# A decode backward kernel on Trainium2: PSUM tiles of two banks and copies of 1024 columns, with a rearranged opening and tail of its last stage

## The chip, the cores and the metric

The kernel runs on one core of one Trainium2 chip. The metric is the device time of an execution in microseconds (us), median over the timed runs. The executions of a kernel lie within about half a per cent of their median here. PE is the matmul engine (PEld its weight loads), DVE the vector engine, ACT the scalar engine, POOL and SP are here the queues that issue stores and loads. PSUM is the memory that PE writes into. The kernel divides it into eight pieces of 512 float32 values per partition, called banks here (its pools take 2 + 4 + 1 + 1), and none of its matmuls writes to more than one. In this program DVE or ACT copies each product out of PSUM ("copy" below), and the bank is filled again only after that. The granted clock is the speed at which the chip's throttle lets PE run, as a share of full speed.

"The Trainium skill" is a set of notes on the chip. Where a statement rests on it, the page is named, and the text says whether the trace agrees.

## The reference, cut to what matters

The reference is a forward pass of two attention blocks and two MLP blocks that share their weights, with one new token per sequence and a KV cache of 16384 entries, followed by the gradient of everything.

```
B, Sq, D = 2, 1, 1024;  Hq, Hkv, Sk, Dh = 32, 4, 16384, 128;  F = 3584      # bf16
x = A_x
for layer in (0, 1):
    x = x + attention(layernorm(x), k_cache, v_cache, wq, wo)
    x = x + mlp(layernorm(x), w1, b1, w2, b2)
return x, *grads(A_x, k_cache, v_cache, wq, wo, w1, b1, w2, b2)
```

The outputs that matter here are the gradients of the caches, dK and dV (33.6 MB each), those of the weights (dWq, dWo, dW1, dW2, together 31.5 MB), and the gradient of the input, the second output, 4 KB, which comes last in the data flow: it needs the whole dq (the gradient of the queries), then dq times Wq, then a layer-norm backward.

## The kernel before: the parts that are touched

What matters of the change is in the last stage, from about 735 us on. In it, K and V chunks and quarters of Wq are loaded once more, dq of layer 0 is formed, and all of dK, dV and dW is computed, copied and stored. Products go to four PSUM tiles of one bank each, used in turn. The program sends each copy to DVE or ACT, whichever has less work by its own count.

```python
    X = [px([128, 512], F32, "xm%d" % i) for i in range(4)]      # four tiles, one bank each
    def mx():
        return nxt("x", X)                                       # the next of the four

    def evac_cast(dst, src, n):                                  # one copy, on ACT or DVE
        if pick() == "A":
            S.copy(out=dst, in_=src)
            charge("A", 0.17 + n / 1200.0)
        else:
            V.tensor_copy(out=dst, in_=src)
            charge("D", 0.15 + n / 960.0)

    # in dw_units: one unit of a weight gradient = one product, one copy
                        ps = mx()
                        PE.matmul(ps[:], lhsT=xrows[p:p + 4, (j0 + j) * 128:(j0 + j + 1) * 128],
                                  rhs=yrows[p:p + 4, y0 + c0:y0 + c0 + 512], start=True, stop=True, tile_position=(p, 0))
                        evac_cast(sv_[:, j, c0:c0 + 512], ps[:], 512)

    # in kv_pair: half a chunk of dK or dV = eight products into four tiles, four copies
        pss = [mx() for _ in range(4)]
        for b in range(2):
            for r in range(4):
                PE.matmul(pss[r][:, b * 256:(b + 1) * 256], lhsT=blk[32 * r:32 * r + 32, o + 2 * h + b, :],
                          rhs=Qm[32 * r:32 * r + 32, :, :].rearrange("p a b -> p (a b)"), start=True, stop=True,
                          tile_position=(32 * r, 0))
        for r in range(4):
            evac_cast(sv_[:, 2 * h:2 * h + 2, r], pss[r][:].rearrange("p (b t d) -> p b t d", b=2, t=2), 512)
```

The main loop goes in steps; in the traces below, the products of PE and the copies of DVE and ACT run in the program's order. A step transposes two blocks of V, forms score products, up to two halves of dK or dV, then some dW units, then issues loads.

```python
    while 2 * m < NS + 12 or late or fill or late_pe or m <= max(v_at) + 2:
        ...                       # for k in 0, 1: 8 transposes of V and their copy, 8 score products, halves of dK / dV
        sch.run_slot(1)           # dq products of earlier steps
        step_fill(1 if m < NCH else 5)              # five dW units of 512 columns
        pump(NLD + 3 if m < NCH else NLD, 3)        # loads, as far as SBUF tiles are free
        m += 1
    g0 = attn_in_bwd(0, g1, dn0)                    # the serial end: layer-norm backward,
    col_to_row_f32(g0, DJ, out_1..., "o1")          # rows, the store of the second output
```

A load takes an SBUF tile that a store has freed, if there is one, and otherwise one that a reader has freed (`(by_store or by_read).popleft()`).

Of the kernel before, what the change touches and what calls it, by code (L numbers as in the profile page):

```python
# [23 lines left out]
def kernel(  # L24
# [65 lines left out]
    ps_x = ctx.enter_context(tc.tile_pool(name="ps_x", bufs=4, space=PSUM))  # L90
    ps_acc = ctx.enter_context(tc.tile_pool(name="ps_acc", bufs=1, space=PSUM))
    ps_sm = ctx.enter_context(tc.tile_pool(name="ps_sm", bufs=1, space=PSUM))

# [30 lines left out]
    zero1 = const.tile([128, 1], F32, name="zero1")  # L124
    V.memset(zero1[:], 0.0)
# [69 lines left out]
    def col_to_row_f32(colT, J, dram_out, name):  # L195
        row = wrk.tile([2, J * 128], BF16, name=name + "_row", tag="rowout")
        for j0 in range(0, J, 4):
            ps = pm_([2, 4, 128], F32, name)
            for j in range(4):
                PE.transpose(ps[0:2, j, :], colT[:, j0 + j, :], identf[:])  # L200
            V.tensor_copy(out=row[:, j0 * 128:(j0 + 4) * 128], in_=ps[0:2, :, :].rearrange("p a b -> p (a b)"))
        nc.gpsimd.dma_start(dram_out, row[:])
# [529 lines left out]
    n_all = vec.tile([128, DJ, 4], BF16, name="n_all")  # L732
    o_all = vec.tile([128, HQ, 4], BF16, name="o_all")
    dq_all = vec.tile([128, HQ, 4], BF16, name="dq_all")
    gA_all = vec.tile([128, DJ, 4], BF16, name="gA_all")
    m_all = vec.tile([128, DJ, 4], BF16, name="m_all")
    h_all = vec.tile([128, FJ, 4], BF16, name="h_all")
    dh_all = vec.tile([128, FJ, 4], BF16, name="dh_all")
    gM_all = vec.tile([128, DJ, 4], BF16, name="gM_all")
    V.tensor_copy(out=gM_all[:, :, 2:4], in_=gT4[:])  # L740
# [7 lines left out]
    def attn_layer_fwd(l, xT):  # L748
        y, rstd = ln_fwd(xT[:], f"a{l}")
        V.tensor_copy(out=n_all[:, :, lsl(l)], in_=y[:])  # L750
        qps, _ = w_pass(A_wq, D, HD, "q_ps", xT_bf=n_all[:, :, lsl(l)])
        qT_bf = vec.tile([128, G, 8], BF16, name=f"qT_bf{l}")
        for b in range(2):
            V.tensor_scalar(out=qT_bf[:, b * HKV:(b + 1) * HKV, :].rearrange("p k r -> p (k r)"), in0=qps[:, :, b],
                            scalar1=QSCALE, scalar2=None, op0=ALU.mult)
        rbc = vec.tile([128, G, 8], F32, name=f"rbc{l}")
        oT = vec.tile([128, G, 8], F32, name=f"oT{l}")
        attn_fwd(l, qT_bf, rbc, oT, ALLG)
        for b in range(2):
            V.tensor_copy(out=o_all[:, :, 2 * l + b], in_=oT[:, b * HKV:(b + 1) * HKV, :].rearrange("p k r -> p (k r)"))  # L760
        aps, _ = w_pass(A_wo, HD, D, "a_ps", xT_bf=o_all[:, :, lsl(l)])
        xn = vec.tile([128, DJ, 2], F32, name=f"xA{l}")
        V.tensor_tensor(out=xn[:], in0=aps[:], in1=xT[:], op=ALU.add)
        saved[f"a{l}"] = dict(y=y, rstd=rstd, qT_bf=qT_bf, rbc=rbc, oT=oT)
        return xn

    def mlp_hidden(l, xT):
        y1, rstd1 = ln_fwd(xT[:], f"m{l}a")
        y2, rstd2 = ln_fwd(y1[:], f"m{l}b")
        V.tensor_copy(out=m_all[:, :, lsl(l)], in_=y2[:])  # L770
        hps, _ = w_pass(B_w1, D, F, "h_ps", xT_bf=m_all[:, :, lsl(l)])
# [17 lines left out]
        V.tensor_tensor(out=h_all[:, :, lsl(l)], in0=hh[:], in1=hpre[:], op=ALU.mult)  # L789
# [24 lines left out]
    def mlp_hidden_bwd(l, dhps, ahead=None):  # L814
        d1 = saved[f"m{l}"]["d1"]
        V.tensor_tensor(out=dh_all[:, :, lsl(l)], in0=d1[:], in1=dhps[:], op=ALU.mult)
        if ahead is not None:
            V.tensor_tensor(out=dh_all[:, 4:FJ:5, lsl(l)], in0=d1[:, 4:FJ:5], in1=ahead.dp[:], op=ALU.mult)

    def mlp_in_bwd(l, gT):  # L820
        sv = saved[f"m{l}"]
        _, dmps = w_pass(B_w1, D, F, "dm_ps", gT_bf=dh_all[:, :, lsl(l)])
# [8 lines left out]
    def attn_out_bwd(l, gT):  # L831
        V.tensor_copy(out=gA_all[:, :, lsl(l)], in_=gT[:])
        _, dops = w_pass(A_wo, HD, D, "do_ps", gT_bf=gA_all[:, :, lsl(l)])
        doT_bf = saved[f"a{l}"]["doT_bf"] = vec.tile([128, G, 8], BF16, name=f"doT_bf{l}")
        dof = wrk.tile([128, G, 8], F32, name="dof")
        do_scaled(l, dops, dof)
        do_store(l, dof[:], doT_bf[:])
        delta(l, delta_mm(l, dof))
        return doT_bf
# [74 lines left out]
    fps, dhps = w_pass(B_w2, F, D, "w2a", xT_bf=h_all[:, :, lsl(0)], gT_bf=gM_all[:, :, lsl(1)])  # L914
# [15 lines left out]
    w2b = Ahead(B_w2, F, "w2b", h_all[:, :, lsl(1)], fps)  # L930
# [16 lines left out]
    V.tensor_copy(out=gM_all[:, :, lsl(0)], in_=g2[:])  # L947
    dhps = px([128, 512], F32, "w2b_b")
    turned = 5
    for j in range(4):  # L950
        w2b.products(j, dhps, gM_all[:, :, lsl(0)])
    w2b.spread(gM_all[:, :, lsl(0)])
    w2b.dots(4)
    for j in range(4, FJ):
# [6 lines left out]
        w2b.products(j, dhps, gM_all[:, :, lsl(0)])  # L961
# [86 lines left out]
    _, dmps = w_pass(B_w1, D, F, "dm_ps", gT_bf=dh_all[:, :, lsl(0)],  # L1048
# [13 lines left out]
    V.tensor_copy(out=gA_all[:, :, lsl(0)], in_=g1[:])  # L1062
    dops = px([128, 512], F32, "wob_b")
    for j in range(4):
        wob.products(j, dops, gA_all[:, :, lsl(0)])
    wob.spread(gA_all[:, :, lsl(0)])
# [4 lines left out]
    for j in range(4, wob.J):  # L1071
# [8 lines left out]
        wob.products(j, dops, gA_all[:, :, lsl(0)])  # L1080
# [7 lines left out]
    def rows_unit(srcs, dst, j0):  # L1088

        def u():  # L1090
            tp = mtp()
            n = 0
            for i, (colT, jlo) in srcs.items():
                jn = min(8, colT.shape[1] - jlo)
                n = max(n, jn)
                for j in range(jn):
                    PE.transpose(tp[32 * i:32 * i + 4, j, :], colT[:, jlo + j, :], ident[:], tile_position=(0, 32 * i))  # L1097
            lo, hi = 32 * min(srcs), 32 * max(srcs) + 4
            evac_bf16(dst[lo:hi, j0 * 128:(j0 + n) * 128], tp[lo:hi, 0:n, :].rearrange("p a b -> p (a b)"), n * 128)
# [3 lines left out]
    X = [px([128, 512], F32, "xm%d" % i) for i in range(4)]  # L1103
# [11 lines left out]

    def n_free():
# [4 lines left out]

    def load_tile():
        return (by_store or by_read).popleft()
# [25 lines left out]
    def dw_units(xrows, yrows, i, chunks, y0, ny, out_of):  # L1149

        p = 32 * i
        box = {}
        units = []
        for j0, rb in chunks:
            for j in range(rb):
                for c0 in range(0, ny, 512):
                    def u(j0=j0, rb=rb, j=j, c0=c0):
                        if j == 0 and c0 == 0:
                            box["t"] = new_home()
                        sv_ = box["t"][:, 0:rb * ny].rearrange("p (j n) -> p j n", j=rb)  # L1160
                        ps = mx()
                        PE.matmul(ps[:], lhsT=xrows[p:p + 4, (j0 + j) * 128:(j0 + j + 1) * 128],  # L1162
                                  rhs=yrows[p:p + 4, y0 + c0:y0 + c0 + 512], start=True, stop=True, tile_position=(p, 0))
                        evac_cast(sv_[:, j, c0:c0 + 512], ps[:], 512)
                        if j == rb - 1 and c0 + 512 >= ny:
# [8 lines left out]
    for i in range(NCH, NC + 1):  # L1174
        if i < NC:
            if chunks[i] != (XG, 0):
                jobs.append(("V",) + chunks[i])
            if i % (2 * NCH) == NCH:
# [33 lines left out]
    fill.append(rows_unit({0: (gM_all, 0), 1: (m_all, 0), 2: (gA_all, 0), 3: (n_all, 0)}, rowsB, 0))  # L1212
    for j0 in range(0, HQ, 8):
        srcs = {0: (h_all, j0), 1: (dh_all, j0), 2: (o_all, j0)}
        fill.append(rows_unit({i: v for i, v in srcs.items() if j0 < v[0].shape[1]}, rowsA, j0))
# [9 lines left out]
    late, late_pe = deque(), deque()  # L1225
# [7 lines left out]
    def kv_pair(w, i, h):  # L1233
# [7 lines left out]
        pss = [mx() for _ in range(4)]  # L1241
        for b in range(2):
            for r in range(4):
                PE.matmul(pss[r][:, b * 256:(b + 1) * 256], lhsT=blk[32 * r:32 * r + 32, o + 2 * h + b, :],  # L1244
                          rhs=Qm[32 * r:32 * r + 32, :, :].rearrange("p a b -> p (a b)"), start=True, stop=True,
                          tile_position=(32 * r, 0))
        for r in range(4):
            evac_cast(sv_[:, 2 * h:2 * h + 2, r], pss[r][:].rearrange("p (b t d) -> p b t d", b=2, t=2), 512)
# [12 lines left out]

    def quarter(kv):

        quarters[kv][1]()
        late_pe.append(quarters[kv][3])
        late.append(rows_unit({3: (dq_all, kv * 8)}, rowsA, kv * 8))
# [43 lines left out]
    def score0(s):  # L1310
# [7 lines left out]
        if c == 0:  # L1318
            open_dq(g)
            if order.index(g) % 2 == 1:  # L1320
                quarter_loads(g % HKV)
        ds0(i, dps["t"][:])
        sch.later(1, lambda: dq_quad(i, 0))
        sch.later(2, lambda: dq_quad(i, 1))
        if c == NCH - 1:
            sch.later(2, accs[g].evac)
            sch.later(3, accs[g].reduce)

    def step_fill(n):
        for k in range(n):  # L1330
            for q in ((late, fill) if k % 2 == 0 else (fill, late)):
                if q and q[0].ready():
# [6 lines left out]

    def fixed_tp(i):  # L1340
        t = pt([128, 8, 128], BF16, "tpm%d" % i)
        S.copy(out=t[:].bitcast(F32), in_=zero1[:].to_broadcast([128, 512]))
        return t
# [21 lines left out]
    odp = {1: kept_scores(1, sm_dp())}  # L1365
# [4 lines left out]
    odp[0] = kept_scores(0, tp_dp())  # L1370
# [6 lines left out]
    odp[3] = kept_scores(3, sm_dp())  # L1377
# [9 lines left out]
    TP.extend(fixed_tp(i) for i in range(2))  # L1387
# [3 lines left out]
    pump(NLD + 3, 4)  # L1391
# [5 lines left out]
    NS = (NC - NCH) * NB  # L1397
    m = 0
    while 2 * m < NS + 12 or late or fill or late_pe or m <= max(v_at) + 2:
# [6 lines left out]
        for k in range(2):  # L1406
# [17 lines left out]
            if late_pe and (k == 1 or s >= NS):  # L1424
                late_pe.popleft()()
            at, w, m_ = ((k_at, "K", m - 1), (v_at, "V", m))[k]
            for h in range(2):
                if at.get(m_ - h) is not None:
                    kv_pair(w, at[m_ - h], h)
        for f in qs:  # L1430
            f()
# [3 lines left out]
        step_fill(1 if m < NCH else 5)  # L1435
        pump(NLD + 3 if m < NCH else NLD, 3)
        m += 1
    g0 = attn_in_bwd(0, g1, dn0)
    col_to_row_f32(g0, DJ, out_1.rearrange("b s d -> (b s) d"), "o1")
# [30 lines left out]
```

## Time and profile before

The median was 1144.42 us of 3 runs.

| reading of before | value | where |
|---|---|---|
| bytes moved, mean rate | 449.30 MB, 394 GB/s | first page, DMA |
| busy share PE / DVE / ACT | 84% / 56% / 50% | first page, part 1 |
| DMA rate 735 to 820 / 820 to 1100 / 1100 to end | 328 / 422 / 298 GB/s | windows |
| a copy of 512 columns, DVE / ACT | 686 / 594 ns | groups of instructions |

These are lines of the first page of before: busy time of each engine, then, in 40 equal slices of the span, the clock granted to PE in tenths of full speed, the busy share of the DMA engines in tenths, and the rate.

```profile
PE 954.6 (84%) x17567; PEld 736.6 (65%) x17567; DVE 633.4 (56%) x1347; ACT 566.2 (50%) x1418; POOL 64.7 (6%) x117
PEclk9989785597999876999998899989779868896785
DMA  9999999998999989999999999887999999999996
GB/s 371 424 424 424 425 423 413 408 379 354 423 424 424 425 302 424 410 377 407 373 423 419 349 354 355 314 331 309 400 423 422 421 420 422 423 422 421 424 419 247
```

The rate runs at a plateau of 420 to 425 GB/s over many slices. The Trainium skill, "DMA: Bandwidth & Descriptors", section "Where 436 GB/s comes from", gives 435 GB/s as the ceiling of the ports; this plateau is just below it. So over the plateau DMA is the limit. The last stage begins near slice 26: it has a slow opening (314, 331, 309), a plateau, and a short slow tail.

These are stretches of the last stage of before, in one line each: window, its length, busy us (and instructions) of PE, PEld, DVE, ACT and POOL, granted clock, DMA busy share, GB/s.

```profile
735.00:755.00 20.00, 16.54 (x280) 12.68 (x280) 10.62 (x24) 10.33 (x20) 1.12 (x2) 0.83 0.71 273
755.00:800.00 45.00, 38.99 (x608) 25.94 (x608) 38.20 (x67) 35.59 (x69) 6.65 (x12) 0.94 0.83 323
...
820.00:1100.00 280.00, 253.25 (x3281) 155.95 (x3277) 215.73 (x374) 201.34 (x387) 42.46 (x71) 0.81 1.02 422
...
1110.00:1120.00 10.00, 7.42 (x53) 3.79 (x52) 5.80 (x12) 4.89 (x9) 1.04 (x2) 0.50 0.83 348
1120.00:1130.00 10.00, 8.85 (x92) 3.96 (x92) 5.94 (x11) 6.06 (x11) 1.83 (x3) 0.50 0.50 206
```

The line for 820 to 1100 us: DMA is full, PE is busy for 253 of 280 us and DVE and ACT for 77% and 72%.

This is a piece of the timeline of before on that plateau: start, length, engine, line, operation, written tile<-read tiles, shape, count, and in brackets the idle time of the engine before it and what ended it. L1162 are dW products, L163 and L166 copies on ACT and DVE. Weight loads are left out.

```profile
844.04 1.07 ACT L163 CAST keepK<-xm 128x512 bf16<-128x512 f32 x2 [0.62 <-PE xm L1244]
844.18 1.28 DVE L166 CAST keepK<-xm 128x512 bf16<-128x512 f32 x2
...
844.68 0.37 PE L1162 MATMUL xm<-rowsA,rowsB 4*128 4x512 bf16 x1 [0.25 <-ACT keepK L163]
...
844.91 0.37 PE L1162 MATMUL xm<-rowsB,rowsA 4*128 4x512 bf16 x1
...
845.09 0.59 ACT L163 CAST keepV<-xm 128x512 bf16<-128x512 f32 x1
...
845.17 1.07 PE L1162 MATMUL xm<-rowsA,rowsB 4*128 4x512 bf16 x3
...
845.57 0.59 ACT L163 CAST big<-xm 128x512 bf16<-128x512 f32 x1
845.58 1.39 DVE L166 CAST keepV<-xm 128x512 bf16<-128x512 f32 x2
...
846.05 0.60 ACT L163 CAST keepK<-xm 128x512 bf16<-128x512 f32 x1
```

The copies follow each other while PE works on. Two copies of 512 back to back take 1.07 us on ACT and 1.28 us on DVE: less than twice 594 and 686 ns, since the second starts before the first is over.

### The profile page before, as it was taken

The numbers are of one execution on the slowest core, as the hardware profiler recorded it, in microseconds if no ns is written. First come the engines' busy times: TensorE is split into PE (matmuls) and PEld (weight loads), VectorE is DVE, ScalarE is ACT, GpSimd is POOL, SyncE is SP. The second block draws the span as 40 slices with busy tenths as digits, with TensorE's granted clock in tenths as the row PEclk, the third lists the DMA queues.
The fourth block names the chain that finished last, engine by engine and source line by source line (L and its number), as shares of the span: only waits on it lengthen the run. The fifth ranks groups of instructions, "written<-read, shape, count | busy, mean of one in ns | idle before, by whom it ended". The sixth has DMA issues, their size and how long they took to land. (4 is left out here: it accounts for less than half of the span.)

```text
span 1140.8 us, 39972 instructions
## 1 busy us (share of the span) xinstructions
PE 954.6 (84%) x17567; PEld 736.6 (65%) x17567; DVE 633.4 (56%) x1347; ACT 566.2 (50%) x1418; POOL 64.7 (6%) x117
## 2 busy tenths in 40 slices
PE   4988896487879885899987789988898989999885
PEld 3867674387767765888776688765555555555552
DVE  1535442133545433544845355768678868786784
ACT  0534351022535330344554444668677767776673
POOL 0000000000000000000000000001111112111111
PEclk9989785597999876999998899989779868896785
DMA  9999999998999989999999999887999999999996
GB/s 371 424 424 424 425 423 413 408 379 354 423 424 424 425 302 424 410 377 407 373 423 419 349 354 355 314 331 309 400 423 422 421 420 422 423 422 421 424 419 247
DMA packets 89130, 449.30 MB, mean 394 GB/s; under 512 B 7026, under 2 KB 7026, under 8 KB 49788
## 3 DMA queue, kind: packets, MB, share of 16 engines
q1 hardware_dynamic: 72204, 348.17, 75.4%
q0 software_dynamic: 16752, 98.59, 20.8%
q8 instruction: 137, 2.24, 0.7%
q14 instruction: 37, 0.30, 0.1%
HBM read 348.14 MB, written 98.58 MB: 392 GB/s over the span
## 5 line engine op out<-in xcount | busy, mean ns | idle before, releaser
L155 ACT COPY kT<-tp 128x512 int32<-128x512 int32 x209 | 122.8, 587 | 252.0 <-PE tp L421 243.3
L158 DVE COPY kT<-tp 128x1024 bf16<-128x1024 bf16 x159 | 108.6, 691 | 109.2 <-PE tp L421 97.3
L421 PE MATMUL tp<-ident,kv_K 128*128 128x128 bf16 x1728 | 144.5, 233 | 4.5 <-DMA kv_K<-in_A_k_cache_dram 4.4
L421 PEld LDWEIGHTS <-kv_K 128*128 128x128 bf16 x1728 | 109.6, 104 | 5.3 <-DMA kv_K<-in_A_k_cache_dram 5.2
L166 DVE CAST big<-xm 128x512 bf16<-128x512 f32 x135 | 88.1, 686 | 25.3 <-PE xm L1162 11.7
L163 ACT CAST big<-xm 128x512 bf16<-128x512 f32 x162 | 88.3, 594 | 24.6 <-PE xm L1162 12.7
L574 PEld LDWEIGHTS <-kT 128*128 128x128 bf16 x2048 | 76.6, 98 | 27.8 <-issue 21.4
L574 PE MATMUL sc<-qT_bf,kT 128*128 128x8 bf16 x2048 | 92.0, 171 | 0.3 <-issue 0.3
L538 ACT ACTIVATE e_all<-sc,negm 128x64 bf16<-128x64 f32 x256 | 77.1, 345 | 1.1 <-DVE negm L533 1.0
L307 PEld LDWEIGHTS <-wt 128*128 128x128 bf16 x1696 | 49.2, 104 | 43.7 <-issue 14.8
L421 PE MATMUL tp<-ident,kv_V 128*128 128x128 bf16 x864 | 70.1, 227 | 8.5 <-DMA kv_V<-in_A_v_cache_dram 7.6
L271 PE MATMUL wtp<-ident,wt 128*128 128x128 bf16 x928 | 73.9, 225 | 3.7 <-issue 2.5
L166 DVE CAST keepK<-xm 128x512 bf16<-128x512 f32 x91 | 59.1, 686 | 21.7 <-PE xm L1244 17.7
L453 PE MATMUL acc_all<-kv_V,e_all 128*16 128x256 bf16 x864 | 46.5, 296 | 26.4 <-DMA kv_V<-in_A_v_cache_dram 13.7
L163 ACT CAST keepK<-xm 128x512 bf16<-128x512 f32 x105 | 56.8, 594 | 23.8 <-PE xm L1244 23.1
L158 DVE COPY wT<-wtp 128x1024 bf16<-128x1024 bf16 (+1 forms) x64 | 40.7, 641 | 46.6 <-PE wtp L271 43.5
L155 ACT COPY wT<-wtp 128x512 int32<-128x512 int32 (+1 forms) x60 | 34.3, 572 | 61.7 <-PE wtp L271 47.5
L421 PEld LDWEIGHTS <-kv_V 128*128 128x128 bf16 x864 | 55.4, 102 | 10.7 <-DMA kv_V<-in_A_v_cache_dram 8.3
L166 DVE CAST keepV<-xm 128x512 bf16<-128x512 f32 (+1 forms) x80 | 52.5, 686 | 16.3 <-PE xm L1244 12.8
L163 ACT CAST keepV<-xm 128x512 bf16<-128x512 f32 (+1 forms) x93 | 50.3, 593 | 20.1 <-PE xm L1244 18.2
L538 ACT ACTIVATION_READ_ACCUMULATOR e_all<-sc,negm 128x1 f32 x256 | 60.1, 235 | 0.0
L271 PEld LDWEIGHTS <-wt 128*128 128x128 bf16 x928 | 56.3, 100 | 4.4 <-issue 3.0
(350 smaller groups left out, 1786.9 us busy)
## 6 DMA issues: line engine op xcount, KB each, us to landing
kv_K<-in_A_k_cache_dram SPq DMA_DIRECT2D x81, 1024.0 KB, 12.3
kv_V<-in_A_v_cache_dram SPq DMA_DIRECT2D x81, 1024.0 KB, 12.1
out_dram<-big POOLq DMA_DIRECT2D x36, 1024.0 KB, 18.5
wt<-in_A_wo_dram SPq DMA_DIRECT2D x32, 1024.0 KB, 10.2
wt<-in_B_w_dram SPq DMA_DIRECT2D x32, 896.0 KB, 14.2
out_dram<-keepK POOLq DMA_DIRECT2D x21, 1024.0 KB, 18.3
out_dram<-keepV POOLq DMA_DIRECT2D x19, 1024.0 KB, 15.0
wt<-in_A_wq_dram SPq DMA_DIRECT2D x16, 1024.0 KB, 9.0
```

Of the source, the lines that this page charges most:

```text
L155: S.copy(out=dst.bitcast(I32), in_=src.bitcast(I32))
L158: V.tensor_copy(out=dst, in_=src)
L163: S.copy(out=dst, in_=src)
L166: V.tensor_copy(out=dst, in_=src)
L271: PE.transpose(tp[:, o, :], wv[:, j, (o0 + o) * 128:(o0 + o + 1) * 128], ident[:])
L307: PE.matmul(fps[:, jo, :].rearrange("p (a b) -> p a b", b=2), lhsT=wv[:, j, jo * 128:(jo + 1) * 128], rhs=xT_bf[:, j0 + j, :].unsqueeze(1) ...
L421: PE.transpose(tp[:, j, :], cv[:, b * 8 + j, :], ident[:])
L453: PE.matmul(self.acc[cg:cg + 16, :], lhsT=coef(u), rhs=self.cv[:, t:t + 2, :].rearrange("p t d -> p (t d)"), start=False, stop=True, tile_ ...
L538: S.activation(out=e_all[:, g, f * half:(f + 1) * half, l, h, :], in_=sc[g][f][:, h, :].rearrange("p (a b) -> p a b", b=2), func=ACT.Exp, ...
L574: PE.matmul(sc[g][f][:, :, t % TH], lhsT=kT[:, j, :], rhs=q_bf[:, g, :], start=True, stop=True)
```

## The change

The intent was four things in the last stage. (1) Products of 1024 columns go to two tiles of two banks each, and one copy takes both banks, to save a start-up per copy. (2) Opening: loads take the tiles that the first dq products have freed, so that they issue earlier, and two Wq loads are moved later. (3) dW units come at an even rate (2 or 3 units of 1024 per step for five of 512), and 3 in the last steps. (4) Tail: the last two groups of dq products come in one slot, the input-gradient chain runs beside the last dWq, and the last dWq uses operands that are zero-padded to all 128 partitions. Smaller edits, such as zero-padded column buffers and the PSUM tiles of the first score products, are left out here. The core of the diff, with cuts:

```diff
-    X = [px([128, 512], F32, "xm%d" % i) for i in range(4)]
+    x_ctx.close()
+    ps_xx = ctx.enter_context(tc.tile_pool(name="ps_xx", bufs=2, space=PSUM))
+    XX = [ps_xx.tile([128, 2, 512], F32, name="xx%d" % i, tag="xx") for i in range(2)]
+    X = [XX[i // 2][:, i % 2, :] for i in range(4)]
...
+    def mxx():
+        rot["x"] += rot["x"] % 2
+        rot["x"] += 2
+        return XX[(rot["x"] - 2) // 2 % 2]
...
     def load_tile():
-        return (by_store or by_read).popleft()
+        return (by_read or by_store if opening["on"] else by_store or by_read).popleft()
...  # dw_units
-                for c0 in range(0, ny, 512):
+                for c0 in range(0, ny, 1024):
-                        ps = mx()
-                        PE.matmul(ps[:], ...)
-                        evac_cast(sv_[:, j, c0:c0 + 512], ps[:], 512)
+                        ps = mxx()[:].rearrange("p a n -> p (a n)") if w > 512 else mx()
+                        for c in range(c0, c0 + w, 512):
+                            PE.matmul(ps[:, c - c0:c - c0 + 512], ...)
+                        evac_cast(sv_[:, j, c0:c0 + w], ps[:, 0:w], w)
...  # kv_pair
-        pss = [mx() for _ in range(4)]
+        pss = [mxx() for _ in range(2)]
-                PE.matmul(pss[r][:, b * 256:(b + 1) * 256], ...)
+                PE.matmul(pss[r // 2][:, r % 2, b * 256:(b + 1) * 256], ...)
-        for r in range(4):
-            evac_cast(sv_[:, 2 * h:2 * h + 2, r], ..., 512)
+        for r in range(2):
+            evac_cast(sv_[:, 2 * h:2 * h + 2, 2 * r:2 * r + 2]..., pss[r]..., 1024)
...  # tail
+        if kv == order[-1] % HKV:
+            tail.extend(in_rows(quarters[kv], kv))            # input-gradient chain, beside dWq
+            late.append(rows_unit({3: (dq_all, kv * 8, HQ)}, qz, 0, 4))
+            late.extend(dw_units(nz, qz, None, [(0, 4), (4, 2), (6, 2)], 0, D, ...))   # zero-padded
-        sch.later(2, lambda: dq_quad(i, 1))
+        sch.later(end, lambda: dq_quad(i, 1))                 # end = 1 for the last chunk
...
-        step_fill(1 if m < NCH else 5)
+        step_fill(1 if m < NCH else 3 if m >= MF else 2 + m % 2, 0)
```

## The prediction

> What bounds the kernel. The profile's first parts show a span of 1140.8 us (1144.4 us timed) and 449.3 MB of DMA traffic, at 420 to 425 GB/s in most slices. At 424 GB/s the bytes alone take about 1060 us, so some 80 us is time in which the DMA engines were not full. DMA limits; PE (84%), DVE (56%) and ACT (50%) do not. The Trainium skill ("DMA: Bandwidth & Descriptors", "Where 436 GB/s comes from") gives 435 GB/s as the port ceiling; the plateau of 424 agrees.
>
> The diff touches only the last stage (from about 730 us: dK, dV, dWq and the other dW). Five-us windows of before give its lost DMA time (missing bytes over 424 GB/s):
> - opening, 735 to 820 us: 184 to 362 GB/s in most windows, about 19 us lost;
> - steady part, 820 to 1110 us: 417 to 430 GB/s, about 1 us lost, though DVE and ACT are 65 to 90% busy;
> - tail, 1110 us to the end: 292 then 33 GB/s in 1115 to 1125, only a 4 KB store after 1136: about 12 us lost.
>
> Opening: the timeline of the load queue shows seven loads between 740 and 793 us, and its waits show them blocked on landing stores (52 + 14 us), since a load prefers tiles freed by a store. The change takes the K tiles that the first dq products have freed (about 736 to 739 us): five loads should issue near 737 to 741 instead of 740 to 782. I expect 10 us of the 19 back (4 to 15).
>
> Tail: last ds product at 1102, last dq quad 1111, reduce 1115, dq cast 1116.4, rows 1118, then all of dWq with four-row products at a granted clock of 0.50 (0.43 us each), then the layer-norm chain and out_1 from 1130 to 1137, serial. The change does both last quads in one slot (about 4 us), runs the input-gradient chain beside dWq, and leaves more stores (four dK/dV, three dWq) after the last dq. I expect the last large store, a dK/dV one, near 1125 and the end near 1131 on the old clock: 6 to 9 us back, limited by the remaining bytes.
>
> Two-bank copies: 512-column casts take 686 ns (DVE) and 594 ns (ACT). Estimate, with 0.53 and 0.43 us for the columns: 1.22 and 1.02 us for 1024, saving 0.16 us per pair; over some 340 pairs 55 us of engine time on two engines. Nearly all of it lies in the DMA-full part and is worth nothing; it may help at 775 to 790 us (DVE 90 to 100% busy). Cost: two double banks rotate instead of four single ones, so PE waits longer for a bank; absorbed.
>
> Zero-padded products: the skill ("TensorE: Matmul & The Clock Gate", Part 1) says activity releases the throttle; the tail's 0.50 agrees that it throttles there. If full rows raise the clock, 0.43 us falls to about 0.22; worth 1 us at most, since casts bound that stretch.
>
> Sum: 10 + 7 = 17 us, device time about 1127 us, 1.5% faster. Range 1116 to 1136. Faster by over 2%: 0.30; within 2%: 0.68; slower: 0.02.
>
> What would show it: windows of 735 to 755 at 400 GB/s or more; steady windows near 422; no 10-us hole in DMA near the end; out_1's store beside the last dK/dV store; 1024-column casts near 1.2 and 1.0 us; bytes unchanged.
>
> What would make it wrong: the opening is limited by copies, not by free tiles, so early loads only move the hole to 760 to 790; double banks starve DVE and ACT enough to open holes in the steady part; or both places gain fully, passing 2%.

## The result, and the profile after

The changed kernel took 1197.63 us (1194.7 to 1198.85, 4 runs), before beside it 1144.13. The ratio is 1.0458, with a 95% interval of 1.042 to 1.0497: slower by 4.6%. Ratios in this text are the mean time of one kernel's fast runs over that of the other's of the same rounds, so they are not quite the ratio of the medians quoted.

The bytes are the same (449.27 MB). Lines of the first page of after, as above:

```profile
PE 971.1 (81%) x17567; PEld 749.4 (63%) x17567; DVE 621.2 (52%) x1177; ACT 559.7 (47%) x1222; POOL 68.0 (6%) x120
PEclk9988795589978967999987999878687768776785
DMA  9999999989999989999998999879999999998965
GB/s 373 423 425 424 424 424 412 404 314 424 424 424 420 402 327 415 373 393 377 422 419 331 360 355 342 332 271 382 369 371 339 393 422 385 347 376 341 406 248 212
```

DVE and ACT are a little less busy, as intended, yet PE's busy time rose for the same 17567 products, and the plateau of the last stage is gone: over slices 30 to 38 it reads 339 to 422 where before had 420 to 424. The same stretches as before:

```profile
735.00:755.00 20.00, 16.53 (x354) 12.66 (x351) 12.19 (x22) 11.57 (x14) 1.12 (x2) 1.00 0.92 359
755.00:800.00 45.00, 35.41 (x476) 22.69 (x475) 28.73 (x35) 28.02 (x37) 4.34 (x9) 0.77 0.71 269
...
820.00:1100.00 280.00, 231.17 (x2795) 142.42 (x2793) 177.84 (x219) 170.07 (x213) 39.56 (x64) 0.75 0.96 373
```

The span grew by 55 us (1140.8 to 1196.0). At 422 GB/s, the 49 GB/s missing between 820 and 1100 us are 13.7 MB, or 33 us; the 12 GB/s missing between 735 and 820 are 1.0 MB, or 2 us; the rest, about 20 us, is almost all lost after 1100 us, where the same behaviour goes on until the tail.

Within the 280 us, PE did 2795 products in 231.17 us where it did 3281 in 253.25. Its idle time rose from 26.8 to 48.8 us, and the mean product from 77.2 to 82.7 ns (busy time over count), at a granted clock of 0.75 for 0.81. At the old mean the missing 486 products would take 37.5 us: 22 us of these are idle time of PE, and 2795 times 5.5 ns, or 15 us, slower products. (Over the whole program, with the same 17567 products, PE's busy time rose by 16.5 us.) In after, the chain of work that ended last, traced from the end, runs through these 280 us in 569 pieces, most of them of PE and the copies, which speaks for PE and the copies setting the pace there; in before it breaks off close to the end, so the two can't be compared. The DMA engines' busy share fell less (1.02 to 0.96) than their rate (422 to 373 GB/s); why was not looked into.

The timeline of after, at about the same time (L1185 are dW products, L162 and L165 copies on ACT and DVE; weight loads left out):

```profile
843.02 1.01 ACT L162 CAST big<-xx 128x1024 bf16<-128x1024 f32 x1 [2.08 <-PE xx L1268]
843.11 1.22 DVE L165 CAST big<-xx 128x1024 bf16<-128x1024 f32 x1 [0.48 <-PE xx L1268]
...
844.08 0.59 PE L1185 MATMUL xx<-rowsA,rowsB 4*128 4x512 bf16 x2 [0.68 <-ACT big L162]
...
844.39 0.59 PE L1185 MATMUL xx<-rowsB,rowsA 4*128 4x512 bf16 x2
...
844.71 1.01 ACT L162 CAST keepV<-xx 128x1024 bf16<-128x1024 f32 x1 [0.68 <-PE xx L1185]
845.01 1.22 DVE L165 CAST keepxK<-xx 128x1024 bf16<-128x1024 f32 x1 [0.68 <-PE xx L1185]
845.77 1.01 PE L1185 MATMUL xx<-rowsA,rowsB 4*128 4x512 bf16 x2 [0.79 <-ACT keepV L162]
```

PE waits 0.68 us for a copy, then both copy engines wait 0.68 us for PE, then PE waits 0.79 us for a copy. They take turns instead of overlapping. A copy of 1024 columns can't start before the second bank is filled, and PE can't put a product into the first bank before the copy of both is done.

The view of the PSUM tiles (xm before, xx after) sums, for all instructions that read or write it after 740 us, the idle time of an engine just before them and what ended it (us, times). The first two lines are copies that waited for dK/dV products and for dW products. Before:

```profile
  PE xm L1244: 97.1, 141
  PE xm L1162: 30.6, 57
```

After:

```profile
  PE xx L1268: 111.5, 179
  PE xx L1185: 111.5, 119
```

The copies' waiting for dW products went from 31 to 112 us. In the other direction, the waits of PE for copies of these tiles, added up over the lines of the wait view, come to 19.7 us between 820 and 1100 us before and to 47.3 us after. That two engines each wait longer for the other is what a hand-over in larger pieces would do; but it is so far a reading of a trace, and several other parts of the change could have caused it.

### The profile page after: what moved, and what is told of

It is laid out like the page before. It is cut to its first block, busy times and chain, and to the rows that moved or that the text cites. A ratio compares the mean times of both kernels' runs of the same rounds, so it can differ in the third digit from the quotient of the medians.

```text
span 1196.0 us, 39477 instructions
## 1 busy us (share of the span) xinstructions
PE 971.1 (81%) x17567; PEld 749.4 (63%) x17567; DVE 621.2 (52%) x1177; ACT 559.7 (47%) x1222; POOL 68.0 (6%) x120
## 2 busy tenths in 40 slices
DMA packets 89142, 449.27 MB, mean 376 GB/s; under 512 B 7042, under 2 KB 7042, under 8 KB 49804
## 4 chain that ended last, share of the span: by engine, by line
PE 57%; DMA 21%; DVE 10%; ACT 8%; issue 3%; POOL 1%; POOLq 0%; DVEq 0%; ACTq 0%
DMA kv_V<-in_A_v_cache_dram 10%; PE tp L421 10%; PE tpm L1464 6%; PE xx L1185 5%; PE xx L1268 5%; PE wtp L271 5%; PE acc_all L453 4%; DMA wt<-in_A_wo_dram 3%; PE dp L1328 3%; PE sc L574 3%; DMA kv_K<-in_A_k_cache_dram 3%; DMA wqt<-in_A_wq_dram 3%; PE turn L323 2%; ACT big L162 2%; PE dp L673 2%
## 5 line engine op out<-in xcount | busy, mean ns | idle before, releaser
L165 DVE CAST big<-xx 128x1024 bf16<-128x1024 f32 (+2 forms) x66 | 77.5, 1174 | 36.0 <-PE xx L1185 15.3
L162 ACT CAST big<-xx 128x1024 bf16<-128x1024 f32 (+1 forms) x71 | 70.4, 995 | 45.4 <-PE xx L1268 26.3
L271 PE MATMUL wtp<-ident,wt 128*128 128x128 bf16 x928 | 76.5, 230 | 3.5 <-issue 2.2
L162 ACT CAST keepV<-xx 128x1024 bf16<-128x1024 f32 (+2 forms) x57 | 56.6, 998 | 33.0 <-PE xx L1268 25.6
L165 DVE CAST keepV<-xx 128x1024 bf16<-128x1024 f32 (+2 forms) x49 | 58.9, 1201 | 23.8 <-PE xx L1268 15.2
L453 PE MATMUL acc_all<-kv_V,e_all 128*16 128x256 bf16 x864 | 46.0, 293 | 27.4 <-DMA kv_V<-in_A_v_cache_dram 13.7
L162 ACT CAST keepK<-xx 128x1024 bf16<-128x1024 f32 (+1 forms) x50 | 49.7, 997 | 32.2 <-PE xx L1185 20.1
L165 DVE CAST keepK<-xx 128x1024 bf16<-128x1024 f32 (+1 forms) x40 | 47.9, 1197 | 25.4 <-PE xx L1268 13.9
L1328 PE MATMUL dp<-wdo,kT 128*128 128x64 bf16 x896 | 60.9, 223 | 0.0
```

The lines of the kernel that those rows point to most:

```text
L271: PE.transpose(tp[:, o, :], wv[:, j, (o0 + o) * 128:(o0 + o + 1) * 128], ident[:])
L453: PE.matmul(self.acc[cg:cg + 16, :], lhsT=coef(u), rhs=self.cv[:, t:t + 2, :].rearrange("p t d -> p (t d)"), start=False, stop=True, tile_ ...
L1328: PE.matmul(dp[:, :, t:t + 4], lhsT=kT[:, j, :], rhs=wd[:, :, x:x + 4], start=(b + j == 0), stop=False)
```

## The experiments

The theory after reading the trace: the two-bank tiles are the loss, since the pair of banks is handed over whole. Rivals: other parts of the change (fewer dW units at one time, the opening, the tail, the padding) cause it; the long copy itself is the cause; the order in which dK/dV fills the tiles is; or something of a tile that spans two banks other than the hand-over. Fifteen kernels ran; all gave correct results.

| run | what it is | median us | ratio to before [95%] |
|---|---|---|---|
| e1_single | the change with one-bank tiles and copies | 1145.51 | 1.0011 [0.9974, 1.0048] |
| e2_double | before with only the two-bank tiles and copies | 1197.07 | 1.0453 [1.0413, 1.0493] |
| e3_pair_tiles | two-bank tiles, one-bank copies, engines alternating | 1269.07 | 1.1087 [1.1039, 1.1135] |
| e4_fill_order | the change, one pair of dK/dV filled before the other | 1193.09 | 1.0423 [1.0379, 1.0468] |
| e5_same_engine | e1, the two copies of a pair on one engine | 1144.91 | 1.0007 [0.9986, 1.0029] |
| e6_pair_same_engine | e5 on two-bank tiles | 1210.41 | 1.0573 [1.0552, 1.0594] |
| e7_spread | the change, dW units spread over the step | 1296.15 | 1.1328 [1.1303, 1.1353] |
| e8_keep | e1, 12 dW units kept for the tail | 1151.39 | 1.0059 [1.004, 1.0078] |
| e9_no_opening | e1 without the opening part | 1144.01 | 0.9998 [0.9971, 1.0024] |
| e10_no_tail | e1 without the tail part | 1148.45 | 1.0029 [1.0003, 1.0055] |
| e11_dq_early | e1, last dq one step earlier | 1142.05 | 0.998 [0.995, 1.0011] |
| e12_last_pair | e11, last dK/dV one step earlier | 1142.77 | 0.9985 [0.9962, 1.0009] |
| e13_reverse | e14, copies of a pair in reverse order | 1195.56 | 1.046 [1.042, 1.05] |
| e14_aligned | e5, pairs start at tile 0 or 2 | 1148.45 | 1.004 [1.0011, 1.0069] |
| e15_two_singles | e1 with two one-bank tiles for four | 1441.33 | 1.2626 [1.257, 1.2682] |

### Which part: e1_single and e2_double

e1_single takes the two-bank tiles out of the change and leaves all else, also that a dW unit is 1024 columns:

```diff
-    XX = [ps_xx.tile([128, 2, 512], F32, name="xx%d" % i, tag="xx") for i in range(2)]
-    X = [XX[i // 2][:, i % 2, :] for i in range(4)]
+    X = [px([128, 512], F32, "xm%d" % i) for i in range(4)]
...  # dw_units
-                        ps = mxx()[:].rearrange("p a n -> p (a n)") if w > 512 else mx()
                         for c in range(c0, c0 + w, 512):
+                            ps = mx()
+                            PE.matmul(ps[:], ...)
+                            evac_cast(sv_[:, j, c:c + 512], ps[:], 512)
-                        evac_cast(sv_[:, j, c0:c0 + w], ps[:, 0:w], w)
```

> The changed kernel with one-bank copies over four separate one-bank tiles; the order of loads, the pace of dW, the tail and the padded dWq stay. Bank theory (the two-bank copies and the two-bank tiles alone cost the time): the middle of the last stage returns to about 420 GB/s, the time to 1120 to 1140 us, below before. Order theory (the new order and pace of loads and dW starve the DMA queues): stays at 1185 to 1200 us.

e2_double is the converse: before, with the two-bank tiles and copies of the change alone (and its number of dW units per step, since a unit is twice as wide).

> The kernel before with only the two-bank tiles and copies (dW units of 1024 columns at half the count per step). Bank theory: 1180 to 1205 us, 340 to 400 GB/s in the middle of the last stage. Order theory: 1135 to 1150 us.

e1 took 1145.51 us, as before did, and e2 took 1197.07 us, as after did. The line of 820 to 1100 us, first e1, then e2:

```profile
820.00:1100.00 280.00, 249.84 (x3210) 150.47 (x3210) 212.44 (x370) 199.65 (x381) 44.37 (x72) 0.82 1.02 422
```

```profile
820.00:1100.00 280.00, 230.00 (x2792) 141.12 (x2788) 179.74 (x217) 170.03 (x214) 36.48 (x62) 0.76 0.98 380
```

The plateau is back in e1 and gone in e2. e1's time lies outside both of its ranges, though: the theory had it below before, at 1120 to 1140 us, because it still counted on a gain from the other parts. So the two-bank tiles and copies are the whole loss, and the rest of the change is worth nothing that this measurement can tell from zero.

### The copy or the tile: e3_pair_tiles, e5_same_engine, e6_pair_same_engine

e3_pair_tiles keeps the two-bank tiles and copies each bank by itself:

```diff
-                        evac_cast(sv_[:, j, c0:c0 + w], ps[:, 0:w], w)
+                        for c in range(c0, c0 + w, 512):
+                            evac_cast(sv_[:, j, c:c + 512], ps[:, c - c0:c - c0 + 512], 512)
```

> The changed kernel with its two two-bank tiles, but each bank copied by its own 512-column instruction, so the copies are as short as before and a tile comes free only when both halves are copied. If the coarse release of the tiles is the cause: still 1175 to 1205 us. If the long copy itself is (a 1.2-us copy holds DVE or ACT and delays other copies): 1120 to 1150 us.

It took 1269.07 us. This did not tell the theories apart: in its trace a copy of one half on ACT waits for the copy of the other half of the same tile on DVE, so the program orders accesses by the whole tile, and two engines on one tile work one after the other. The next pair avoids that. e5_same_engine is e1 with both copies of a pair on one engine (four one-bank tiles), e6_pair_same_engine the same on two-bank tiles:

```diff
   # e1 to e5
+    def evac_pair(pairs_):
+        e = pick()
+        for dst, src, n in pairs_:
+            (S.copy if e == "A" else V.tensor_copy)(**({"out": dst, "in_": src}))
+        charge(e, ...)
   # e5 to e6
-    X = [px([128, 512], F32, "xm%d" % i) for i in range(4)]
+    XX = [ps_xx.tile([128, 2, 512], F32, name="xx%d" % i, tag="xx") for i in range(2)]
+    X = [XX[i // 2][:, i % 2, :] for i in range(4)]
```

> e1_single with both banks of a pair copied by one engine, one after the other, as in the changed kernel; the banks are still separate tiles that come free one by one. If the coarse two-bank tiles are the cause: 1138 to 1152 us as e1_single. If it is that one engine takes 1024 columns in a row: 1180 to 1205 us.

> The changed kernel's two two-bank tiles, each copied by two one-bank copies of one engine. It differs from e5_same_engine only in the tiles. (e3_pair_tiles mixed in another wait: in its trace ACT's copy of a tile waits for DVE's copy of the same tile.) If the coarse tiles are the cause: 1190 to 1215 us, so close to the 1197 of the long copies. If the long copy is: 1138 to 1155 us.

e5 took 1144.91 us and e6 1210.41 us. The line of 820 to 1100 us, first e5, then e6:

```profile
820.00:1100.00 280.00, 253.10 (x3215) 152.26 (x3212) 209.71 (x365) 199.72 (x384) 44.05 (x71) 0.81 1.02 422
```

```profile
820.00:1100.00 280.00, 227.03 (x2760) 139.14 (x2760) 182.02 (x319) 172.67 (x329) 34.70 (x59) 0.76 0.96 371
```

The copies of e6 have 512 columns, so the long copy is not the cause; on two-bank tiles one copy of 1024 (after, ratio 1.0458) even did better than two of 512 (1.0573). The choice of engine is not the cause either (e5). The tile is. Waits of PE for copies of these tiles sum to 18.0 us in e5 and 51.6 us in e6 in this window. (In e5 a pair can start at any tile, in e6 it can't; e14 below shows that this is worth 0.3%.)

### Order and place of the work: e4_fill_order, e7_spread

e4_fill_order is the change with the eight dK/dV products of a half ordered so that one pair is full before the other is begun:

```diff
-        for b in range(2):
-            for r in range(4):
+        for b, r in ((0, 0), (0, 1), (1, 0), (1, 1), (0, 2), (0, 3), (1, 2), (1, 3)):
```

> The changed kernel, but in dK and dV the four products of one two-bank tile are issued before those of the other, so that its copy can start while the second tile is still held. If waiting for both tiles at once is most of the loss: 1150 to 1180 us; if the loss lies with dW or elsewhere: within 8 us of 1197.

It took 1193.09 us: some 0.3 of the 4.6 per cent, a difference within the intervals. e7_spread is the change with two of the 2.5 dW units of a step moved from its end to its middle:

```diff
+            if m >= NCH:
+                step_fill(1, 0)
...
-        step_fill(1 if m < NCH else 3 if m >= MF else 2 + m % 2, 0)
+        step_fill(1 if m < NCH else 1 if m >= MF else m % 2, 0)
```

> The changed kernel with two of the 2.5 dW units of each step moved between the transposes and the score products instead of at the step's end one after another. If PE, which issues in order, loses its time standing at the second and third dW unit of a step for a two-bank tile: 1160 to 1182 us, with under 25 us of PE idle before dW products (40 us in the changed kernel). If the dW placement does not matter: within 8 us of 1197.

It took 1296.15 us, far outside what was expected of it. The line of 820 to 1100 us:

```profile
820.00:1100.00 280.00, 243.32 (x2163) 123.08 (x2161) 140.01 (x177) 134.36 (x163) 27.33 (x47) 0.57 0.79 293
```

The wait that was to shrink did: PE's idle time before dW products fell from 28.5 us in after to 11.0 us, and all its idle time from 48.8 to 36.7 us. What went wrong is the length of the products: 112 ns in the mean for 83, at a granted clock of 0.57 for 0.75. The copies in turn waited longer for dK/dV products (200 us for 112, after 740 us). So nearly all of e7's further loss is in slower products and not in PE's waits. Why spreading lowers the clock this far was not pursued.

### What of a two-bank tile: e14_aligned, e13_reverse, e15_two_singles

The prediction had been wrong and one point was open: is it the hand-over of both banks at once, or something else of a tile that spans two banks? e14_aligned is the control: e5, four one-bank tiles, where a pair always starts at tile 0 or 2. e13_reverse differs from it in one word:

```diff
   # e14 to e13
-        for dst, src, n in pairs_:
+        for dst, src, n in reversed(pairs_):
```

PE fills the first tile of a pair and then the second. In e13 the engine copies the second first, so it can't start before PE has filled both, and PE's next product, which goes to the first tile, can't start before both copies are done. The hand-over is that of a two-bank tile, but every tile is one bank.

> Control for e13: four one-bank tiles, both copies of a pair on one engine (the kernel that took 1144.9 us), and a pair always starts at tile 0 or 2, as the two-bank tiles do. Every theory: 1141 to 1150 us, ratio 0.997 to 1.006, about 420 GB/s between 820 and 1100 us; the alignment alone skips a tile now and then.

> Four one-bank tiles as in e14, but the engine copies the second tile of a pair first. So its first copy can't start before the last product of the pair has ended, and PE's next product, which goes to the first tile of the pair, can't start before both copies have ended: the pair is handed over whole, though every tile is one bank. Theory (hand-over in pairs is the cost): most of the loss comes back, 1180 to 1215 us, ratio 1.03 to 1.06, 370 to 395 GB/s between 820 and 1100 us, PE waiting on copies 40 us or more in that window. Rival (something else of a tile that spans two banks): as e14, within 0.5% of it.

e14 took 1148.45 us, e13 1195.56 us. The line of 820 to 1100 us, first e14, then e13:

```profile
820.00:1100.00 280.00, 249.51 (x3146) 151.08 (x3139) 206.70 (x360) 196.91 (x380) 43.53 (x70) 0.80 1.02 421
```

```profile
820.00:1100.00 280.00, 227.08 (x2758) 138.96 (x2759) 184.51 (x322) 174.33 (x333) 37.75 (x61) 0.76 0.97 377
```

So the loss is there without a single two-bank tile. The timeline of e13 (L1194 are dW products, L163 copies; other lines left out) shows the same turns as that of after:

```profile
852.29 0.58 PE L1194 MATMUL xm<-rowsA,rowsB 4*128 4x512 bf16 x1 [0.62 <-ACT keepxV L163]
...
853.33 1.07 ACT L163 CAST big<-xm 128x512 bf16<-128x512 f32 x2 [1.09 <-PE xm L1194]
853.65 1.29 DVE L163 CAST keepxK<-xm 128x512 bf16<-128x512 f32 x2 [1.10 <-PE xm L1194]
...
854.45 1.00 PE L1194 MATMUL xm<-rowsA,rowsB 4*128 4x512 bf16 x2 [0.84 <-ACT big L163]
...
855.50 1.07 ACT L163 CAST big<-xm 128x512 bf16<-128x512 f32 x2 [1.09 <-PE xm L1194]
```

ACT waits 1.09 us for PE, PE 0.84 us for ACT, ACT 1.09 us for PE. PE's waits for copies of the tiles sum to 51.6 us in the window, against 21.0 us in e14. The rival, which had e13 within 0.5% of e14, falls as an account of the main loss: the hand-over in pairs alone costs 47 us. It may not be all. e6, which has the same copies as e13 on two-bank tiles, took 1210.41 us (1.0573 against 1.046), so some 15 of the 62 us between e14 and e6 are not accounted for by e13; what they are was not tested.

e15_two_singles is e1 with half of the tiles; the dK/dV products are ordered two tiles at a time.

```diff
-    X = [px([128, 512], F32, "xm%d" % i) for i in range(4)]
+    X = [px([128, 512], F32, "xm%d" % i) for i in range(4)][:2]
```

> The change with one-bank copies (1145.5 us with four one-bank tiles) on only two one-bank tiles, engines alternating: half the banks of the two-bank version, but as many separately released tiles. Estimate from the trace: one turn of a tile is a copy (0.64 us in the mean) plus a product (0.37) plus the gaps between them (about 0.25), so two tiles give one bank every 0.63 us, where the two-bank version gave one every 0.45 us at 843 to 847 us and four single tiles one every 0.32. Theory (the rate at which banks are turned round is the cost): slower than the two-bank version, 1230 to 1330 us, ratio 1.07 to 1.16. Rival (the rate is not the cost, spanning two banks is): 1145 to 1195 us.

It took 1441.33 us. The line of 820 to 1100 us:

```profile
820.00:1100.00 280.00, 228.57 (x1828) 116.17 (x1826) 128.26 (x210) 120.30 (x211) 22.34 (x38) 0.52 0.67 246
```

The direction is that of the theory, but the loss is larger than its range. The estimate had a product at 0.37 us; here the clock was 0.52 and a dW product took 0.58 us in the median. PE waited for copies of the tiles for 49.6 us, no longer than in e13 (51.6), but it did 1828 products for 2758, at 125 ns in the mean for 82. So in this window most of what e15 lost beyond e13 is slower products. That the waits are what lowers the clock is not shown by a run.

### What the opening and the tail are worth: e9_no_opening, e10_no_tail

Both are e1 less one part. e9 takes out the opening (which tiles loads take, when the first Wq quarter is loaded, a count of spare tiles), e10 the tail (one slot for the last dq groups, the chain beside dWq, the padding).

```diff
   # e9
-        return (by_read or by_store if opening["on"] else by_store or by_read).popleft()
+        return (by_store or by_read).popleft()
-            if i % (2 * NCH) == NCH + (2 if i < 2 * NCH else 0):
+            if i % (2 * NCH) == NCH:
   # e10
-        if kv == order[-1] % HKV: ...      # the early chain and the padded dWq
-        end = 1 if i == NC - 1 else 2
+        end = 2
```

> e1_single without the opening part (loads again take store-freed tiles first, the first wq loads come early, the spare of the first pump is 4 again); one-bank copies, pace and tail stay. The prediction put 10 us on the opening: by it, 1151 to 1158 us. If early loads only move the hole in DMA traffic from 740-755 to 755-800 us (as e1_single's windows show): within 4 us of e1_single (1141 to 1149).

> e1_single without the tail part (last dq over two steps, dWq of the last quarter as the others, input gradient and output 1 after the loop). The prediction put 7 us on the tail: by it, 1149 to 1155 us. If the copies and stores left after the last dq set the end (e1_single's last dq is 4 us closer to its last ds, its end is not earlier): 1142 to 1148 us.

e9 took 1144.01 us (ratio 0.9998, e1 had 1.0011): the opening part is worth nothing measurable. e10 took 1148.45 us (1.0029), between its two expected ranges: the tail part is worth some 0.2%, 2 to 3 us, and the intervals of e1 and e10 overlap, so this is not told from zero. The stretches of e1, first of its opening, then of its tail, to be read against those of before, show why:

```profile
735.00:755.00 20.00, 16.78 (x331) 12.13 (x328) 13.17 (x29) 11.62 (x23) 1.28 (x3) 1.00 0.84 324
755.00:800.00 45.00, 40.30 (x561) 25.69 (x559) 35.01 (x61) 33.15 (x65) 6.48 (x12) 0.85 0.84 300
...
1110.00:1120.00 10.00, 7.27 (x47) 3.74 (x45) 5.41 (x11) 4.21 (x9) 1.06 (x2) 0.50 0.88 369
1120.00:1130.00 10.00, 8.46 (x98) 3.84 (x94) 6.76 (x14) 6.64 (x13) 1.50 (x3) 0.67 0.36 145
```

In the opening, the rate of the first 20 us rose from 273 to 324 GB/s, and that of the next 45 us fell from 323 to 300: over 735 to 820 us it is 326 against 328. The first four loads did issue at 736.1 to 739.7 us (740.7 to 749.0 before), but the next ones at 760.9, 775.7 and 787.7, where before had 761.7, 782.6 and 793.1. The hole in the loads moved and kept its size.

In the tail, the copy of dq came 10.1 us after the multiplication that follows the last score product (14.1 before), so the intended 4 us were won there. But that multiplication came 2.7 us later than before (1104.7 us for 1102.0), and from dq to the end of the span it took 26.3 us, where it took 24.6: in these two executions nothing is left of the 4 us. The DMA hole is deeper (145 GB/s for 206), and six stores are issued after 1125 us, where before had four.

### Trying to keep the tail busy: e8_keep, e11_dq_early, e12_last_pair

e8_keep is e1 with the last 12 dW units kept back, to have stores while the chain of dq runs:

```diff
-        step_fill(1 if m < NCH else 3 if m >= MF else 2 + m % 2, 0)
+        step_fill(1 if m < NCH else 3 if m >= MF else 2 + m % 2, 12 if 2 * m < NS - 2 else 0)
```

> e1_single with the last 12 dW units (3 MB of stores) kept back until the last loads are in, to fill the hole in DMA traffic near 1117 to 1126 us of e1_single. If the last 25 us are limited by DMA work that comes too late: 1132 to 1140 us. If they are limited by the chain from dq to dWq and the input gradient: 1143 to 1150 us.

It took 1151.39 us, slower than e1 and just outside both expected ranges. e11_dq_early is e1 with the last dq groups in the step of the last score product, and its reduction half a step later; e12_last_pair moves in addition the last dK and dV chunk one step forward.

```diff
   # e11
-        end = 1 if i == NC - 1 else 2
-        sch.later(1, lambda: dq_quad(i, 0))
+        end = 0 if i == NC - 1 else 2
+        sch.later(min(1, end), lambda: dq_quad(i, 0))
   # e12
-    v_at = {2 * i - 3: i for i in range(2, NC)}
-    k_at = {(i if i < NCH else 2 * i - NCH): i for i in range(NC)}
+    v_at = {2 * i - 3 - (i == NC - 1): i for i in range(2, NC)}
+    k_at = {(i if i < NCH else 2 * i - NCH - (i == NC - 1)): i for i in range(NC)}
```

> e1_single with the last dq products at the end of the step of the last ds and their reduction after the first dK half of the next step, so that dq should be ready some 4 us earlier. If the chain to dq sets the end: 1138 to 1142 us. If the copies and stores left set it: 1142 to 1148 us.

> The change with one-bank copies and the last dq group and its reduction early (the kernel that took 1142.05 us), and the products, copies and stores of the last chunk's dK and dV one step earlier, so that their stores are issued ahead of the store of the second output and not behind it (there they were issued at 1129.74 and 1131.51 us, the output's store at 1126.50, the end at 1138.6). Theory: the end of that kernel is set by these two late stores, so it ends 4 to 9 us earlier: 1132 to 1139 us, ratio 0.988 to 0.995 to before. Rival: the tail moves a fixed number of bytes through a DMA queue that is already as full as its issue allows, so advancing two stores moves the hole and nothing else: 1139 to 1145 us, ratio 0.995 to 1.001.

e11 took 1142.05 us (ratio 0.998), e12 1142.77 us (0.9985). In e11 the store of the second output was issued at 1126.5 us, 10 us earlier than before, but two large stores followed at 1129.7 and 1131.5 us and set the end. In e12 the order of the last stores changed, yet a last large store was issued at 1135.0 us. The rival of e12 held: moving these stores moved the hole. Both have medians below that of before, but the intervals include 1, so no version is shown to beat before.

## Why the prediction was wrong, point by point

- **What bounds the kernel** was read rightly for before: DMA on a plateau of 422 GB/s in the last stage. It did not hold for after (373 GB/s).
- **The step that failed** is the one on the cost of two double banks: "two double banks rotate instead of four single ones, so PE waits longer for a bank; absorbed". It was not absorbed. PE was busy for 253 of 280 us there, so it had 27 us of slack in all, and its waits for copies alone rose by 28 us (19.7 to 47.3). e2 shows that this part alone costs 4.5%, e6 that the length of the copy is not what costs, and e13 that the hand-over in pairs costs as much (4.6%) with one-bank tiles.
- **A second loss came with it.** The granted clock of PE fell from 0.81 to 0.75, and its products took longer (15 of the 37 us reckoned above). The Trainium skill, "TensorE: Matmul & The Clock Gate", section "A second HAM failure mode: psum-queue depth-cycling", describes that short idle times of PE between groups of matmuls, from cycling through PSUM banks, throttle its clock; the traces agree in direction: 0.81 to 0.82 in before, e1 and e5, 0.75 to 0.76 in after, e2, e6 and e13, 0.52 in e15. The sum of the idle time does not settle it, though: e7 had less of it than after (36.7 for 48.8 us) and a clock of 0.57. The prediction cited that page for the tail alone. No run changed the clock alone, so its share is an estimate.
- **The saving of the long copy** was taken as 0.16 us per pair of 512. The lengths were predicted well (1.22 and 1.01 us). But two copies of 512 back to back take 1.28 us on DVE and 1.07 us on ACT in before, so the saving is 0.06 us per pair. The term was too large by more than twice, and lay where the prediction itself called it worth nothing. The Trainium skill had both halves of this in "Perfetto Trace Analysis", section "Optimizing Scalar/DVE Operations": that the profiled length of such an instruction holds about twice the fixed cost that occupies the engine, since the end of one overlaps with the next, and that larger operations help where the engine is saturated, while where DVE and ACT are not saturated but cause bubbles on other engines, smaller ones may be better. DVE and ACT were 77% and 72% busy in before, and the runs agree with the second case only where the tiles are split as well: e1, with short copies and one-bank tiles, got the loss back, e6, with short copies on two-bank tiles, did not. The prediction did not look that page up.
- **The opening**, "10 us of the 19 back", gave none (e9). The early loads came, the rate of 400 GB/s in 735 to 755 us did not (359 in after, 324 in e1), and the hole moved to the following 45 us. That is what the prediction had listed under what would make it wrong; what exactly limits the loads there is left open.
- **The tail**, "6 to 9 us", gave 2 to 3 us, not told from zero (e10). The 4 us for dq were won, but 2.7 us were lost ahead of it and 1.7 us after it, and the last large store was issued at 1133.8 us where before had 1131.2.
- **The padded products** were to run faster if full rows raised the clock. They hardly did: in the tail of after they took 0.61 us in the median (all 128 partitions full, clock 0.61 from 1170 to 1186 us), and before's sixteen four-row products there took 0.63 us (clock 0.50 from 1118 to 1131 us).
- **The chances**: 0.02 for slower was far too sure. "Double banks starve DVE and ACT enough to open holes in the steady part" stood in the list of what could go wrong, and no number was put to it. An estimate was possible from before's trace and the prediction's own lengths: a turn of a two-bank tile is a copy (1.12 us in the mean), two products (0.60 us: one takes 0.37, and the next starts 0.23 after it) and the waits between them, so two such tiles give a bank every 0.43 us at best ((1.12 + 0.60) / 4), when copy and fill of one tile follow each other strictly. Four one-bank tiles with copies of 0.64 us and products of 0.37 us allow one every 0.25 us (1.01 / 4). After's turn at 843 us was 1.69 us on ACT and 1.90 on DVE, 0.45 us per bank; in before nine banks were copied between 844.04 and 846.97 us, one every 0.33 us. So in such a burst before took banks faster than two-bank tiles give them. Over the whole 280 us it made 547 copies from these tiles, one every 0.51 us, so the limit binds in the bursts alone: the estimate gives the direction, not the size of the loss.

Still open: what limits the loads of the opening; what lowers the clock, above all where dW units are spread (e7); what e6 lost beyond e13; and how the loss splits between waits and clock.

## What to carry to other kernels

Before several small PSUM tiles are joined into fewer large ones, reckon how often a bank comes back: copy plus fill plus the gaps, over the number of tiles that are released separately. Where the engine that fills and the engines that copy were as busy as here (90%, 77% and 72% of the stage), the number of separate hand-overs was worth more than a shorter copy, and even the order of two copies decides it (47 us here for one reversed loop). On a stage at the DMA ceiling, price what a change costs the other engines against their slack there, not only what it saves.

## What the Trainium skill lacked or had wrong

- "Perfetto Trace Analysis", sections "Matmuls" and "Matmul Optimizations", says that groups should rotate through different PSUM banks and that all eight should be in use. Before and after both use four banks in rotation in this stage; what differed was how many pieces are handed over separately. The page lacks that: 1148.45 against 1195.56 us with the same banks and only the order of two copies reversed.
- The same page, section "Optimization Strategy", says that consistent bubbles can mean that there isn't enough PSUM for the next tile, and names buffer count and tile sizes. The runs agree (waits of PE for copies 19.7 against 47.3 us from 820 to 1100 us), and add that the gaps show on both sides at once, since the copies' waits for dW products grew too (31 to 112 us, after 740 us).
- The same page, section "Optimizing Scalar/DVE Operations", puts the fixed cost of a copy out of PSUM at about 125 ns on DVE and 51 ns on ACT. Merging two copies into one saved about 60 ns on each (1.28 against 1.22 us on DVE, 1.07 against 1.01 on ACT): ACT agrees, for DVE the page has about twice what was saved here. Its advice to break up instructions that cause bubbles on other engines held here only together with separate tiles (e1 against e6); what it lacks is that a copy can be small and the bubble stay all the same, if the copies are issued in an order that hands over two banks together (e13).
- "TensorE: Matmul & The Clock Gate", "A second HAM failure mode: psum-queue depth-cycling", gives no size. Here the mean granted clock went from 0.81 to 0.75 with 22 us more idle time in 280 us, and to 0.52 in e15; but it was 0.57 in e7, with 12 us less idle time than after. That full rows raise the clock, as the prediction tried on the ground of Part 1, was hardly seen: padded products took 0.61 us, four-row ones 0.63.
